# Attention and a gated feed-forward layer on one core: block means of the first batch's values from the windows of the first eight halves, with a new order list for the opening

## The chip, the cores and the metric

One core of one Trainium2 chip runs the kernel. Its engines are PE (matrix products; its weight loads are shown apart as PEld), DVE (vector), ACT (scalar functions), POOL (GpSimd) and SP, which here only issues transfers. The metric is the device time of one launch in microseconds (us), as a median over several runs. A hardware profile of one execution is at hand as well, and its span and rows are what the text argues from.

## The reference

Attention over 4 batches, 8 heads, 768 positions and 64 values a head. Every position sees a band of keys near it, and for each block of 32 positions one maximum of its keys and one mean of its values. The result passes through two dense layers with a rational function between them.

```python
k_sum = k.reshape(B, H, nb, block, D).max(axis=3)       # block = 32, nb = 24
v_sum = v.reshape(B, H, nb, block, D).mean(axis=3)
scores_l = where(|i - j| < 16, scale * q @ k.T, -1e9)
scores_s = scale * q @ k_sum.T + log(block)
a = softmax(concatenate([scores_l, scores_s], axis=-1))
x = a @ concatenate([v, v_sum], axis=2)
...
h = x @ w_in                                            # 3072 x 512 by 512 x 2048
P = a[0] + a[1] * h + a[2] * h**2 + a[3] * h**3
Q = 1.0 + |b[0]| * |h| + |b[1]| * h**2
out = (P / (Q + 1e-06)) @ w_out
```

## The kernel before

**Halves.** Attention works on 64 query positions of all eight heads at a time, a *half*; there are 48, twelve to a batch, and eight make the 512 rows of a *group* for the dense layers (six groups). A half uses a window of 96 keys and values (its 64 positions and 16 on either side) and the 24 block values of its batch, 120 rows in all. Its steps, in `half`, `softmax`, `turned` and `values`, are: scores on PE (`one_scores`, or `both_scores` for two halves at once where `PAIRS` has a 1), mask and minimum on DVE, exponentials on ACT, reciprocal on DVE, scaling on POOL, four transposes on PE (`turned`, with `FILL` matmuls without use ahead of them), a copy of the transposed rows (`ENG_P` says on which engine), the product with the values on PE, and the output split into a high part `xh` (`ENG_X`) and a rest `xl`.

**Names in the profile.** `sc` scores, `ss` attention rows, `sm` their minima and sums, `pt` and `pts` the transposed rows, `vw`, `vr` and `vlast` the value windows with their block means in rows 96 to 119, `av` the product, `vf` whole tiles of values and the sums over them, `kres` keys, `qres` queries, `ks` block maxima, `kw` the keys of one half, `wr` raw weights, `wearly` and `w` split weights, `h` the first layer's result, `ta`, `tq`, `tu`, `gh`, `gl` the rational function, `po` the second layer's result. `pt<-mask,ident` are the filling matmuls.

**Block means of the first batch.** The rows 96 to 119 of the eight windows of halves 0 to 7 (`vres`) hold the same 24 means. `value_tiles(0)` loads the batch's 768 value rows as six tiles of 128, in one transfer of four and one of two. Six accumulating matmuls (`value_average`, tokens v0 to v5) multiply them by the constant `avg`, which holds 1/32 in the right places. `first_means` (token m) copies the result into `vres`: three copies on ACT, five on POOL. The second batch's means are made in the same way (`u`, `n`). The windows themselves are loaded by `load_v` (tokens V).

**Steps.** A step is a first-layer block of 512 rows by 128 columns (`moe1`, tokens x, three parts of four matmuls), the rational function in nine parts (`gelu`, tokens ga to gk), and a second-layer part (`moe2`, tokens y). 96 steps make up the run, sixteen to a group. Weights come as 64-bit words and are turned into a high and a low part (`w_split`, tokens w).

**Order.** Up to first-layer step 13 the order is a list written out in `TEXT`. Each token advances one chain by one piece, and a wrapper around the engines makes each engine take its instructions in the order of the list. Capital letters issue loads from SP: K keys, Q queries, V value windows, F and G value tiles of the first and second batch, W weights, A queries and keys of later halves, I keys of the second batch; `S` loads the small constants. k and i make block maxima on DVE. After the list a loop goes on with steps 14 to 95.

Of the kernel before, what the change touches and what calls it, by code (L numbers as in the profile page):

```python
# [8 lines left out]
F32 = mybir.dt.float32  # L9
# [4 lines left out]
ALU = mybir.AluOpType  # L14
# [8 lines left out]
P = 128  # L23
# [24 lines left out]
TEXT = ("K0 K2 k0 K1 Q0 k1 k2 K3 k3 S0 Q1 F0 W0 V0 V1 V2 A9 V3 V5 V6 V7 W1 V4 W2 W3 h0 A8 G0 h0 h0 h1 h1 h0 h3 h1 h2 h0 h4 h6 h1 h2 h4 v0 h5 h0 h1 h1 h3 h4 h2 h0 h3 h6 h2 h2 h0 h2 "  # L48
# [11 lines left out]
AVGW = NK + NB - 4  # L60
NLATE = 4
# [6 lines left out]
PAIRS = "11001000"  # L68
SMODE = "xxxxxxxxxxxxxxxx"
ENG_P = "dddddaadaaaaaaaa"  # L70
ENG_X = "daadaaaaaaadaaaa"
MODE = "ccccceceeccccccc"
SQ_PS = "001001001001110"
PRODUCT = "00000000000000"
FILL = "0000000040200000"
TREE = "0000"
KDMA = "00000000"
# [4 lines left out]
def tile_kernel(ctx, tc, qw_in, kraw, kwin, vpad, vred, wio, a, b, cmask, cident, cavg, out):  # L82
# [52 lines left out]
    kfull = wm.tile([P, NPAIR * SPAD + AVGW], F32, tag="wm", name="kres")  # L135
    kres = kfull[:, 0:NPAIR * SPAD].rearrange("p (r s) -> p r s", r=NPAIR)
    avg = kfull[:, NPAIR * SPAD:]

# [52 lines left out]
    def value_tiles(bi):  # L191
        vt = []
        for i, (n, pool, tag) in enumerate(((4, xp, "xh"), (2, stage if bi else xp, "st" if bi else "xl"))):
            t = pool.tile([P, n, DM], F32, tag=tag, bufs=2, name=f"vf{bi}_{i}")
            syn.dma_start(out=t, in_=vpad[bi, WIN + 4 * i * P:WIN + (4 * i + n) * P, :].rearrange("(t p) e -> p t e", p=P))
            vt += [t[:, k, :] for k in range(n)]
        return vt

    order = {"v": 0, "m": 0}

    def value_average(av, vt, i):
        assert order["v"] % len(vt) == i
        order["v"] += 1
        pe.matmul(av[:NK, :], avg[:, AVGW - NK - 4 * i:AVGW - 4 * i], vt[i], start=(i == 0), stop=(i == len(vt) - 1))

    def first_means(av):
        assert order["v"] == 6
        order["m"] += 1
        for t in vres[0:3]:
            act.copy(t[NKW:NK, :], av[NKW:NK, :])  # L210
        for t in vres[3:]:
            gps.tensor_copy(t[NKW:NK, :], vw[0][NKW:NK, :])

    def second_means(av):
        order["m"] += 1
        t = pp.tile([NK, DM], F32, tag="p", name="vn")
        act.copy(t[NKW:NK, :], av[NKW:NK, :])
        syn.dma_start(out=vnext, in_=t[NKW:NK, :])
# [55 lines left out]
    def softmax(jj, sc):  # L274
# [31 lines left out]
        for pr in range(NPAIR):  # L306
            gps.tensor_scalar(ss[:, pr, 0:NK], ss[:, pr, 0:NK], sm[:, 1, pr:pr + 1], 1.0, op0=ALU.mult, op1=ALU.mult)
# [4 lines left out]
    def half(jj):  # L312

        other = jj ^ 1
        pair = PAIRS[jj // 2] == "1"
        if jj >= HPG:
            for k in (min(jj, other), max(jj, other)) if pair else (jj,):
                if k not in paired:
                    paired.add(k)
                    key_blocks(k)  # L320
            yield
        if jj not in score_tiles:
            if pair:
                score_tiles[min(jj, other)], score_tiles[max(jj, other)] = both_scores(min(jj, other))
            else:
                score_tiles[jj] = one_scores(jj)
            scored.update((jj, other) if pair else (jj,))
        yield
        yield from softmax(jj, score_tiles[jj])
        yield  # L330
        lead(turned(jj, jj < HPG), True)
        yield
        yield from values(jj, jj < HPG)

    def load_v(jj):
        bi, j = divmod(jj, NJ)
        vt = vres[jj] if jj < HPG else vw[jj % 2]
        assert jj < HPG + 2 or jj - 2 in finished
        syn.dma_start(out=vt[0:NKW, :], in_=vpad[bi, j * HQ:j * HQ + NKW, :])
        if j < 2 and bi == 1:  # L340
            assert order["m"] == 2
            syn.dma_start(out=vt[NKW:NK, :], in_=vnext)
        elif j < 2 and bi > 1:
            nc.gpsimd.dma_start(
                out=vt[NKW:NK, :].rearrange("n (q d) -> n q d", q=4),
                in_=vsum[bi].rearrange("p c e -> p (c e)"))

    finished, facing = set(), {}
# [307 lines left out]
    def token(kind, n):  # L656
# [29 lines left out]
        elif kind == "F":  # L686
            syn.dma_start(out=avg, in_=cavg)
# [3 lines left out]
        elif kind == "v":  # L691
            if n == 0:
                tiles["v"] = ps_a.tile([P, DM], F32, tag="a", name="vf")
            value_average(tiles["v"], tiles["f", 0], n)
        elif kind == "m":
            first_means(tiles["v"])
        elif kind == "u":
            if n == 0:
                tiles["u"] = ps_o.tile([P, DM], F32, tag="o", name="vf1")
            value_average(tiles["u"], tiles["f", 1], n)  # L700
# [49 lines left out]
def _layout(q, k, v, moe_w_in, moe_w_out, moe_a, moe_b):  # L750
# [27 lines left out]
    avg = np.zeros((P, AVGW), f)  # L778
    avg[np.arange(P), NKW + NB - 4 + np.arange(P) // BLK] = 1.0 / BLK
    return {  # L780
# [23 lines left out]
```

## Time and profile before

| what | value |
|---|---|
| median of three runs | 642.35 us (641.74 to 643.24) |
| the profiled execution | 641.28 us |
| its span | 639.5 us |
| PE busy | 621.2 us, 97% |
| DVE busy | 567.8 us, 89% |
| ACT busy | 460.2 us, 72% |
| POOL busy | 256.0 us, 40% |
| PE's granted clock | 1.00 |
| moved by DMA | 78.58 MB |

Busy times are unions of an engine's instructions. A row of the view of instructions in order of time gives start, duration, engine, line, operation, output and inputs, shape and count, and in brackets the idle time ahead and what ended it. Almost every row has the line of the wrapper, 110, so rows are told apart by their tiles. PE takes matmuls in a pipeline, so the distance between two starts, and not a duration, is what one costs there; an fp32 matmul shows as two.

### The profile page before, as it was taken

How to read it: one execution, taken by the hardware profiler on the slowest of the kernel's cores; microseconds unless marked ns; L12 is line 12 of the kernel's file. 1: busy time of each engine (PE TensorE's matmuls, PEld its weight loads, DVE VectorE, ACT ScalarE, POOL GpSimd, SP SyncE). 2: the span in 40 equal slices, each digit the busy share in tenths (PEclk: the TensorE clock that was granted, in tenths of full speed). 3: DMA queues.
4: the chain of work that ended last, by engine and by line, in shares of the span. 5: the costliest groups of instructions: out<-in, count | busy, mean ns of one | idle time of the engine just before them, and what ended most of it. 6: DMA issues, size and time to landing. Idle time of an engine off the chain costs nothing.

```text
span 639.5 us, 11900 instructions
## 1 busy us (share of the span) xinstructions
PE 621.2 (97%) x4080; PEld 497.0 (78%) x4080; DVE 567.8 (89%) x1152; ACT 460.2 (72%) x1032; POOL 256.0 (40%) x353
## 2 busy tenths in 40 slices
PE   8799999999999999999999999999999999999997
PEld 5566777778788878888888878888888888888886
DVE  5689989999989999989988989988988988898885
ACT  3989999978777767777767677667786775656652
POOL 1838768663243244243243234244234232222221
PEclk9999999999999999999999999999999999999999
DMA  9997856504534424333424442223342210100001
GB/s 319 302 353 259 260 161 207 193 27 138 164 122 140 132 81 139 114 114 127 143 79 121 123 145 89 86 92 98 86 143 85 72 64 1 55 12 2 0 2 66
DMA packets 52136, 78.58 MB, mean 123 GB/s; under 512 B 6132, under 2 KB 33396, under 8 KB 50156
## 3 DMA queue, kind: packets, MB, share of 16 engines
q1 hardware_dynamic: 50796, 75.67, 36.4%
q0 software_dynamic: 560, 1.77, 1.5%
q8 instruction: 32, 0.52, 0.3%
q10 hardware_dynamic: 720, 0.38, 0.2%
q14 instruction: 28, 0.23, 0.1%
HBM read 61.31 MB, written 14.73 MB: 119 GB/s over the span
## 4 chain that ended last, share of the span: by engine, by line
PE 72%; DVE 13%; ACT 6%; issue 3%; DMA 3%; POOL 2%; DVEq 0%; POOLq 0%; ACTq 0%
PE po L110 33%; PE h L110 31%; DVE tu L110 4%; PE sc L110 3%; DVE tq L110 3%; PE av L110 3%; ACT ta L110 2%; POOL ss L110 2%; DVE gh L110 2%; DMA kres<-in_kraw_dram 1%; ACT ss L110 1%; PE pt L110 1%; DVE vs L110 1%; DMA w<-wr 1%; PE vf L110 1%
## 5 line engine op out<-in xcount | busy, mean ns | idle before, releaser
L110 POOL TENSOR_TENSOR gl<-tu,ta 128x512 fp32r<-128x512 f32 x96 | 129.6, 1350 | 299.8 <-DVE tu L110 177.6
L110 ACT ACTIVATE ta<-tq,cs 128x512 f32<-128x512 f32 x96 | 69.6, 725 | 87.6 <-DVE tq L110 86.7
L110 PE MATMUL po<-wearly,gh 128*128 128x512 f32 x384 | 121.1, 397 | 0.9 <-ACT o L110 0.9
L110 POOL TENSOR_SCALAR ss<-ss,sm 128x120 f32<-128x120 f32 x192 | 94.6, 510 | 65.7 <-DVE sm L110 62.3
L110 PE MATMUL po<-w,gh 128*128 128x512 f32 x384 | 119.9, 394 | 0.0
L110 PE MATMUL h<-xh,wearly 128*128 128x512 f32 x384 | 97.4, 393 | 0.5 <-ACT xh L110 0.5
L110 PE MATMUL h<-xh,w 128*128 128x512 f32 x384 | 96.5, 391 | 1.3 <-DVE tu L110 1.0
L110 PEld LDWEIGHTS h<-xh,w 128*128 128x128 f32 x384 | 71.8, 188 | 16.9 <-ACT ta L110 1.4
L110 PEld LDWEIGHTS po<-wearly,gh 128*128 128x128 f32 x384 | 70.5, 188 | 18.2 <-ACT o L110 2.5
L110 PEld LDWEIGHTS h<-xh,wearly 128*128 128x128 f32 x384 | 71.9, 188 | 16.4 <-issue 0.7
L110 PEld LDWEIGHTS po<-w,gh 128*128 128x128 f32 x384 | 71.2, 188 | 15.6 <-issue 1.3
L110 DVE SCALAR_TENSOR_TENSOR gh<-tu,cs,ta 128x512 fp32r<-128x512 f32 x96 | 72.8, 759 | 11.7 <-ACT ta L110 2.2
L110 ACT ACTIVATE ss<-ss,sm 128x120 f32<-128x120 f32 x192 | 73.2, 384 | 12.7 <-DVE sm L110 12.5
L110 PE MATMUL po<-w,gl 128*128 128x512 f32 x192 | 75.0, 390 | 0.0
L110 PE MATMUL po<-wearly,gl 128*128 128x512 f32 x192 | 75.0, 390 | 0.0
L110 ACT ACTIVATE tu<-h,cs 128x512 f32<-128x512 f32 x96 | 74.6, 777 | 0.2 <-PE h L110 0.2
L110 DVE SCALAR_TENSOR_TENSOR tu<-tu,cs,tq 128x512 f32<-128x512 f32 x96 | 72.2, 752 | 2.7
L110 DVE SCALAR_TENSOR_TENSOR tu<-tu,cs,h 128x512 f32<-128x512 f32 x96 | 71.1, 740 | 2.2
L110 DVE SCALAR_TENSOR_TENSOR tq<-tq,gh 128x512 f32<-128x512 f32 x96 | 67.0, 698 | 2.7
L110 ACT ACTIVATE ta<-h,cs 128x512 f32<-128x512 f32 x96 | 65.2, 679 | 5.1 <-POOL gl L110 5.1
L110 DVE TENSOR_TENSOR tu<-tu,h 128x512 f32<-128x512 f32 x96 | 64.9, 676 | 1.2 <-ACT tu L110 0.7
L110 ACT ACTIVATE ta<-ta 128x512 f32<-128x512 f32 x96 | 60.8, 633 | 2.7
(78 smaller groups left out, 911.0 us busy)
## 6 DMA issues: line engine op xcount, KB each, us to landing
wr<-in_wio_dram SPq DMA_DIRECT2D x15, 1024.0 KB
cross<-tb SPq DMA_DIRECT2D x32, 256.0 KB
vw<-in_vpad_dram SPq DMA_DIRECT2D x42, 192.0 KB
kw<-in_kwin_dram SPq DMA_DIRECT2D x40, 192.0 KB
pts<-cross SPq DMA_DIRECT2D x96, 64.0 KB
out_dram<-o SPq DMA_DIRECT2D x23, 256.0 KB
qw<-in_qw_dram SPq DMA_DIRECT2D x40, 128.0 KB
kr<-in_kraw_dram SPq DMA_DIRECT2D x12, 384.0 KB
```

Of the source, the lines that this page charges most:

```text
L110: out = getattr(self.engine, name)(*args, **kw)
```

## The change

The first batch's means come from ten matmuls in place of six. Eight take rows 16 to 79 of the windows of halves 0 to 7, once loaded (`window_average`, tokens v0 to v7, with a constant `avgw` of 96 rows); two take the last two whole tiles (`value_average`, v8 and v9), the only ones that are still loaded. `first_means` makes two copies on ACT and six on POOL.

Other settings change with it. `PAIRS`: halves 4 to 7 score in pairs too. `SMODE`: half 1 subtracts its minimum on POOL, takes one exponential for all four blocks and sums on DVE (y); halves 2 to 5 are scaled on DVE by one product over all four blocks (z). `ENG_P`, `ENG_X`: which engine copies. `SQ_PS`: the square of step 1 goes to PSUM. `PRODUCT`: step 0 forms its denominator with two ACT operations and a POOL product. `FILL`: fewer filling matmuls. `KDMA`: the block maxima of half 12 are copied by a transfer. The order list is another one; of it the openings are shown, to about the first x tokens.

```diff
-TEXT = ("K0 K2 k0 K1 Q0 k1 k2 K3 k3 S0 Q1 F0 W0 V0 V1 V2 A9 V3 V5 V6 V7 W1 V4 W2 W3 h0 A8 G0 h0 h0 h1 h1 h0 h3 h1 h2 h0 h4 h6 h1 h2 h4 v0 h5 h0 h1 h1 h3 h4 h2 h0 h3 h6 h2 h2 h0 h2 "
-         "h3 v1 h3 h3 h5 h4 h5 h4 w0 v2 v3 w0 w0 h7 h4 v4 v5 h3 h5 h7 m0 h2 h1 h0 h2 h5 h1 h1 h0 h0 w0 h5 w0 W4 h6 h3 h6 h7 h7 h4 h6 h4 h2 h6 h7 h2 h7 h1 h2 h1 h5 h5 h3 h6 h3 h5 w1 "
...
+TEXT = ("K0 K2 K1 Q0 K3 Q1 k2 V2 k0 V0 F0 V5 S0 k1 V1 k3 h0 h0 W0 V6 h1 V4 h0 V3 h0 h1 V7 W1 A8 h1 A9 h2 h0 h4 h3 h2 h3 v0 v2 h3 h4 h0 h1 h2 h2 h0 h3 h1 h2 v1 h6 h5 h3 h2 w0 W3 h3 "
+         "W2 v5 h4 h6 v9 G0 h0 h5 w0 h4 h4 v8 h1 w0 v6 v4 h5 h5 h4 v3 h7 v7 h1 m0 h0 h5 h2 h5 h7 h7 h3 h1 h2 w0 w0 h6 h0 h0 h6 h6 h4 h3 h2 h2 h7 h1 h1 h2 h6 h5 h5 h3 h5 h3 h7 h1 h4 "
...
+AVGH = NK + NB - 2
+NREST = (S - HPG * HQ) // P
-PAIRS = "11001000"
-SMODE = "xxxxxxxxxxxxxxxx"
-ENG_P = "dddddaadaaaaaaaa"
-ENG_X = "daadaaaaaaadaaaa"
+PAIRS = "11111000"
+SMODE = "xyzzzzxxxxxxxxxx"
+ENG_P = "dddddaadaaaaaada"
+ENG_X = "addaadaaaaddaaaa"
-SQ_PS = "001001001001110"
-PRODUCT = "00000000000000"
-FILL = "0000000040200000"
+SQ_PS = "011001001001110"
+PRODUCT = "10000000000000"
+FILL = "0000000010000010"
-KDMA = "00000000"
+KDMA = "00011000"
+ENG_M = "aagggggg"
...
-        for i, (n, pool, tag) in enumerate(((4, xp, "xh"), (2, stage if bi else xp, "st" if bi else "xl"))):
+        for i, (k, n, pool, tag) in enumerate(((0, 4, xp, "xh"), (4, 2, stage, "st")) if bi else ((S // P - NREST, NREST, xp, "xl"),)):
...
+    def window_average(av, n, jj):
+        assert jj in loaded
         order["v"] += 1
-        pe.matmul(av[:NK, :], avg[:, AVGW - NK - 4 * i:AVGW - 4 * i], vt[i], start=(i == 0), stop=(i == len(vt) - 1))
+        pe.matmul(av[:NK, :], avgw[:, AVGH - NK - 2 * jj:AVGH - 2 * jj], vres[jj][0:NKW, :], start=(order["v"] == 1), stop=(order["v"] == n))
...
-        for t in vres[0:3]:
-            act.copy(t[NKW:NK, :], av[NKW:NK, :])
-        for t in vres[3:]:
-            gps.tensor_copy(t[NKW:NK, :], vw[0][NKW:NK, :])
+        for t, e in zip(vres, ENG_M):
+            if e == "a":
+                act.copy(t[NKW:NK, :], av[NKW:NK, :])
+            else:
+                (dve if e == "d" else gps).tensor_copy(t[NKW:NK, :], vw[0][NKW:NK, :])
...
-        for pr in range(NPAIR):
+        if jj < 2 * HPG and SMODE[jj] == "z":
+            dve.tensor_tensor(ss, ss, sm[:, 1, :].unsqueeze(2).to_broadcast([P, NPAIR, NK]), op=ALU.mult)
+        for pr in range(NPAIR) if jj >= 2 * HPG or SMODE[jj] != "z" else ():
             gps.tensor_scalar(ss[:, pr, 0:NK], ss[:, pr, 0:NK], sm[:, 1, pr:pr + 1], 1.0, op0=ALU.mult, op1=ALU.mult)
...
-            syn.dma_start(out=avg, in_=cavg)
+            syn.dma_start(out=kfull[:, NPAIR * SPAD:], in_=cavg)
```

More of the change, by code (lines that the diff above doesn't have):

```diff
@@ L134, in tile_kernel @@
     qres = wm.tile([P, HPG, NPAIR, HQ], F32, tag="wm", name="qres")
-    kfull = wm.tile([P, NPAIR * SPAD + AVGW], F32, tag="wm", name="kres")
+    kfull = wm.tile([P, NPAIR * SPAD + AVGW + AVGH], F32, tag="wm", name="kres")
     kres = kfull[:, 0:NPAIR * SPAD].rearrange("p (r s) -> p r s", r=NPAIR)
     avg = kfull[:, NPAIR * SPAD:]
+    avgw = kfull[0:NKW, NPAIR * SPAD + AVGW:]
     def setup():
@@ L192, in value_tiles, with value_average @@
         vt = []
-        for i, (n, pool, tag) in enumerate(((4, xp, "xh"), (2, stage if bi else xp, "st" if bi else "xl"))):
+        for i, (k, n, pool, tag) in enumerate(((0, 4, xp, "xh"), (4, 2, stage, "st")) if bi else ((S // P - NREST, NREST, xp, "xl"),)):
             t = pool.tile([P, n, DM], F32, tag=tag, bufs=2, name=f"vf{bi}_{i}")
-            syn.dma_start(out=t, in_=vpad[bi, WIN + 4 * i * P:WIN + (4 * i + n) * P, :].rearrange("(t p) e -> p t e", p=P))
-            vt += [t[:, k, :] for k in range(n)]
-        return vt
-    order = {"v": 0, "m": 0}
-    def value_average(av, vt, i):
-        assert order["v"] % len(vt) == i
+            syn.dma_start(out=t, in_=vpad[bi, WIN + k * P:WIN + (k + n) * P, :].rearrange("(t p) e -> p t e", p=P))
+            vt += [(k + c, t[:, c, :]) for c in range(n)]
+        return vt
+    order = {"v": 0, "m": 0, "u": 0}
+    def value_average(kind, av, n, k, vt):
+        order[kind] += 1
+        pe.matmul(av[:NK, :], avg[:, AVGW - NK - 4 * k:AVGW - 4 * k], vt, start=(order[kind] == 1), stop=(order[kind] == n))
+    def window_average(av, n, jj):
+        assert jj in loaded
         order["v"] += 1
-        pe.matmul(av[:NK, :], avg[:, AVGW - NK - 4 * i:AVGW - 4 * i], vt[i], start=(i == 0), stop=(i == len(vt) - 1))
+        pe.matmul(av[:NK, :], avgw[:, AVGH - NK - 2 * jj:AVGH - 2 * jj], vres[jj][0:NKW, :], start=(order["v"] == 1), stop=(order["v"] == n))
     def first_means(av):
-        assert order["v"] == 6
+        assert order["v"] == HPG + NREST
         order["m"] += 1
-        for t in vres[0:3]:
-            act.copy(t[NKW:NK, :], av[NKW:NK, :])
-        for t in vres[3:]:
-            gps.tensor_copy(t[NKW:NK, :], vw[0][NKW:NK, :])
+        for t, e in zip(vres, ENG_M):
[3 more added lines that the diff above has]
+                (dve if e == "d" else gps).tensor_copy(t[NKW:NK, :], vw[0][NKW:NK, :])
     def second_means(av):
+        assert order["u"] == S // P
         order["m"] += 1
@@ L322, in half @@
         if jj not in score_tiles:
+            assert jj >= HPG or order["k", 0] == NPAIR
             if pair:
@@ L338, in load_v @@
         assert jj < HPG + 2 or jj - 2 in finished
+        loaded.add(jj)
         syn.dma_start(out=vt[0:NKW, :], in_=vpad[bi, j * HQ:j * HQ + NKW, :])
@@ L346, in load_v @@
                 in_=vsum[bi].rearrange("p c e -> p (c e)"))
-    finished, facing = set(), {}
+    finished, loaded, facing = set(), set(), {}
     def turned(jj, early=False):
@@ L691, in token @@
         elif kind == "v":
-            if n == 0:
+            if order["v"] == 0:
                 tiles["v"] = ps_a.tile([P, DM], F32, tag="a", name="vf")
-            value_average(tiles["v"], tiles["f", 0], n)
+            if n < HPG:
+                window_average(tiles["v"], HPG + NREST, n)
+            else:
+                value_average("v", tiles["v"], HPG + NREST, *tiles["f", 0][n - HPG])
         elif kind == "m":
@@ L697, in token @@
         elif kind == "u":
-            if n == 0:
+            if order["u"] == 0:
                 tiles["u"] = ps_o.tile([P, DM], F32, tag="o", name="vf1")
-            value_average(tiles["u"], tiles["f", 1], n)
+            value_average("u", tiles["u"], S // P, *tiles["f", 1][n])
         elif kind == "n":
@@ L777, in _layout @@
         ms.append(np.concatenate([m, m], axis=0))
-    avg = np.zeros((P, AVGW), f)
+    avg = np.zeros((P, AVGW + AVGH), f)
     avg[np.arange(P), NKW + NB - 4 + np.arange(P) // BLK] = 1.0 / BLK
+    rows = np.arange(HQ)
+    avg[WIN + rows, AVGW + NKW + NB - 2 + rows // BLK] = 1.0 / BLK
     return {
```

20 rows, old and new, of the table TEXT are left out of this document.

## The prediction, on record before the changed kernel was timed

> **What bounds the kernel now.** I read the page's span first, then the busy times by stage, then who PE waited for in each stage, then the instructions of each engine in order of time.
>
> ```profile
> span 639.5 us, 11900 instructions
> ...
> 9.00:36.86 27.86, 22.89 (x428) 17.05 (x429) 19.48 (x93) 21.92 (x86) 20.03 (x41) 1.00 1.04 339
> 36.86:139.50 102.64, 98.21 (x613) 73.13 (x614) 98.26 (x193) 94.10 (x188) 68.01 (x61) 1.00 0.65 209
> 139.50:639.50 500.00, 492.86 (x3029) 403.82 (x3027) 446.77 (x864) 342.91 (x758) 167.76 (x248) 1.00 0.29 91
> ```
>
> The columns after the length are the busy times of PE, PEld, DVE, ACT and POOL, then PE's granted clock, the DMA share and GB/s. The order list ends near 139.5 us. Behind it PE is busy for 492.86 of 500.00 us, by code that the change leaves alone. So the change can act in two stages only. **Stage A**, 9.00 to 36.86, is the attention of the first eight halves, up to the first first-layer matmul. No engine is full there: PE idles 27.86 - 22.89 = 5.0 us. **Stage B**, 36.86 to 139.5, interleaves first-layer steps 0 to 13 and second-layer steps 0 to 10 with eight more halves. There PE is busy 98.21 of 102.64 us and DVE 98.26. Both are 96% full and ACT 92%, so taking work from one of them alone need not shorten it.
>
> ```profile
> PE pt L110 <- DVE pts L110: 1.2, 1, 1.2
> ...
> PE av L110 <- DVE xl L110: 0.8, 2, 0.5
> ...
> PE pt L110 <- POOL ss L110: 3.1, 6, 0.9
> PE h L110 <- DVE tu L110: 1.0, 1, 1.0
> ```
>
> The first two rows are waits of PE in stage A (total, times, longest), both for attention's small DVE work. The last two are those of stage B, mostly for POOL scaling the attention rows.
>
> **The change, part by part.** First PE's terms.
>
> ```profile
> 9.04 0.40 PE L110 MATMUL sc<-kres,qres 64*64 64x96 f32 x8 [0.29 <-DMA qres<-in_qw_dram]
> 9.31 0.40 PE L110 MATMUL sc<-kres,qres 64*64 64x96 f32 x8
> ...
> 18.62 2.74 PE L110 MATMUL vf<-vf,kres 128*120 128x512 f32 x6
> 21.29 0.38 PE L110 MATMUL sc<-kres,qres 64*64 64x96 f32 x4
> 21.59 0.36 PE L110 MATMUL sc<-kres,qres 64*64 64x96 f32 x4
> ...
> 51.65 2.58 PE L110 MATMUL pt<-mask,ident 128*128 128x360 f32 x8
> 54.07 0.38 PE L110 MATMUL pt<-ident,ss 128*120 128x128 f32 x2
> 55.33 0.66 PE L110 MATMUL pt<-ident,ss 128*120 128x128 f32 x2 [0.88 <-POOL ss L110]
> ```
>
> The means of batch 0 take ten matmuls (eight windows of 96 rows, two whole tiles) where six stood. Each is two passes of 512 columns; six passes took 21.29 - 18.62 = 2.67, so 0.445 a pass and four more matmuls cost 8 x 0.445 = +3.6 us. No row shows one of 96 rows. By rows they would be 0.75 of it, which makes all ten 2 x 0.445 x (2 + 8 x 0.75) = 7.1 against 5.3 now, +1.8; the upper end is +3.6 with nothing gained for fewer rows. I take +3.6, by the row of equal columns. Halves 4 to 7 now score in pairs: a block of eight passes over the keys and eight over the block maxima takes 9.31 - 9.04 = 0.27 for two halves at once, against 21.59 - 21.29 = 0.30 for four and four of one half alone. A half alone is four such blocks, 1.2 us; a pair is 4 x 0.27 = 1.1. Two pairs in place of four singles save 4 x 1.2 - 2 x 1.1 = 2.6. So PE has +3.6 - 2.6 = +1.0 in stage A. The filling matmuls of the turns fall from six (four at half 8, two at half 10) to two (one at 8, one at 14). Eight passes took 54.07 - 51.65 = 2.42, 0.30 each, so four fewer save 8 x 0.30 = 2.4 in stage B. The four at half 8 now stand in front of a wait that went on for another 0.88 after them, so their removal pays only if the list has other PE work to put there.
>
> Next the engines beside it.
>
> ```profile
> 19.69 1.39 POOL L110 TENSOR_SCALAR ss<-ss,sm 128x120 f32<-128x120 f32 x4 [0.19 <-DVE sm L110]
> ...
> 25.27 1.73 POOL L110 COPY vr<-vw 24x512 f32<-24x512 f32 x3 [0.47 <-ACT vw L110]
> ...
> 30.76 2.75 POOL L110 TENSOR_SCALAR ss<-ss,sm 128x120 f32<-128x120 f32 x8 [0.21 <-DVE sm L110]
> ...
> 51.68 3.93 POOL L110 TENSOR_SCALAR ss<-ss,sm 128x120 f32<-128x120 f32 x4
> ...
> 49.24 0.68 DVE L110 TENSOR_TENSOR tu<-tu,h 128x512 f32<-128x512 f32 x1
> 49.84 0.75 DVE L110 SCALAR_TENSOR_TENSOR tq<-tq,cs,ta 128x512 f32<-128x512 f32 x1
> 50.50 0.74 DVE L110 SCALAR_TENSOR_TENSOR tu<-tu,cs,h 128x512 f32<-128x512 f32 x1
> ...
> 58.09 0.95 DVE L110 TENSOR_REDUCE ks<-kr 128x24 f32<-128x768 f32 x1
> 58.96 0.17 DVE L110 RECIPROCAL sm<-sm 128x4 f32<-128x4 f32 x1
> ...
> 27.86 0.42 DVE L110 CAST xh<-av 128x256 fp32r<-128x256 f32 x1
> 29.90 0.68 DVE L110 COPY pts<-pt 120x512 f32<-120x512 f32 x1
> 39.38 0.32 DVE L110 COPY kw<-ks 128x96 f32<-128x96 f32 x2
> ...
> 24.55 1.06 ACT L110 COPY vw<-vf 24x512 f32<-24x512 f32 x2 [0.93 <-PE vf L110]
> ...
> 30.34 0.19 ACT L110 ACTIVATION_READ_ACCUMULATOR ss<-ss,sm 128x1 f32 x1
> ```
>
> Scaling a half costs POOL 1.39 (four instructions, DVE quiet). Halves 2 to 5 give this to DVE as one product of 128x480. The nearest row, 128x512, starts 0.60 before the next, so I take 0.6 each: DVE +2.4, POOL -4 x 1.39 = -5.6. Half 1 subtracts its minimum on POOL in one instruction (between 0.3, one of the four scalings, and 1.4, all four; I take 1.3, as it covers all four blocks), ACT takes one exponential in place of four with their accumulator reads, and DVE gets a reduction of 480 columns (0.95 for 768, so 0.59) and an addition on four (0.17 as the reciprocal), 0.75; ends 0.34, two of the short ones, and 1.1 (0.95 + 0.17). One mean copy moves from ACT to POOL (1.73 / 3 = 0.58). Three output copies (halves 1, 2, 5) move to DVE and two (0, 3) away, net one of 0.42. So in stage A, DVE has +2.4 + 0.75 + 0.4 = +3.5, with 27.86 - 19.48 = 8.4 idle to hold it; POOL has -5.6 + 1.3 + 0.6 = -3.7.
>
> Where stage A ends is set by the last halves. Now their scalings end at 30.76 + 2.75 = 33.5, and the first layer starts 3.35 later, at 36.86. In the new list PE makes all ten averaging matmuls before the second transpose; I put their end where it is now, near 24.6, since PE has +1.0 more but idles less ahead of it. Then come two ACT copies (24.55 + 1.06 shows them), six POOL copies of 0.58, to about 24.6 + 0.5 + 3.5 = 28.6, and then the scalings of halves 6 and 7. The last exponential stands behind as much ACT work as now and ends near 30.5 (its last read is at 30.34), so half 7 is scaled from 30.5 and done by 31.9 to 32.9 (1.4 alone, up to 2.4 beside a busy DVE). That is 0.6 to 1.6 earlier; I take **-1.1**. What is late next is the ACT and DVE pair of output copies of halves 6 and 7, as now.
>
> Stage B has two ends. If PE sets it, it shrinks by the 2.4 of fills. If DVE sets it, it grows by DVE's own balance: step 0's combination moves to POOL, 49.84 to 50.50, -0.66; one copy of block maxima goes by DMA, 0.32 / 2, -0.16; half 14's transposed copy and half 10's output copy come to it, 0.68 + 0.42; together +0.3. I take **-0.8**, between them: PE's waits here are for POOL (3.1) three times as much as for DVE (1.0), and the list puts first-layer work of step 4 ahead of the first second-layer work, near where the fills stood, which speaks for PE's end; DVE's 98.3 speaks for the other.
>
> Edits that I cost at nothing. The loads:
>
> ```profile
> wr<-in_wio_dram SPq DMA_DIRECT2D x6, 1024.0 KB
> vf<-in_vpad_dram SPq DMA_DIRECT2D x2, 1024.0 KB
> kres<-in_kraw_dram SPq DMA_DIRECT2D x4, 400.0 KB
> qres<-in_qw_dram SPq DMA_DIRECT2D x2, 512.0 KB
> vf<-in_vpad_dram SPq DMA_DIRECT2D x2, 512.0 KB
> vr<-in_vpad_dram SPq DMA_DIRECT2D x4, 192.0 KB
> ...
> 374.76 1.98 DMA cross<-tb
> ...
> 36.14 1.89 POOL L110 TENSOR_SCALAR wr<-wr 128x1024 int32<-128x1024 uint8 x1 [0.17 <-DMA wr<-in_wio_dram]
> ```
>
> Batch 0 drops its 1024 KB tile, some 3.1 us of transfer at the 339 GB/s of stage A. What it relieves is the weights, and the wait for those is 0.17; so nothing is booked. SP's queue takes value windows 2, 0, 5 and 1 ahead of the first weights and the others right behind. The averages now wait for all eight, and behind that wait stand PE's transposes. Ahead of the last window lie keys, queries, eight windows, two tiles and one weight block: 4 x 400 + 2 x 512 + 8 x 192 + 512 + 1024 KB = 5.8 MB, 17.2 us at 339 GB/s. Begun near 2 us and with 1.98 for a landing (the row of a small transfer) at most, they are there by 21.2, while PE reaches the last average near 23.7. The cover is 2.5 us; gone, the means and all behind them come later by what is lacking. The block maxima of half 12 by DMA add an issue on SP, where weights and windows queue behind its wait for the maxima, and a landing of some 1.98; both are covered if the scores stand that far behind, and the loads behind it are several steps early. Step 1's square in PSUM changes the buffer, not the operation.
>
> Sum: -1.1 - 0.8 = -1.9. The profiled execution took 641.28, its span 639.5 and 1.8 around it, so it would come to 639.4. It lies 1.1 below the median of the runs, 642.35, and I forecast a median of **640.4**.
>
> **A rule weighed.** POOL's four scalings took 1.39 at 19.69 and 3.93 at 51.68, where DVE was full: one slows the other. The Trainium skill, SBUF — State Buffer, "SBUF: two separate sides", says that GpSimd and a VectorE operation with two SBUF inputs take the shared port in turn, whole instructions long. The POOL rows agree. By it, the four products on DVE may each wait out a POOL copy, and moving work between those two need not help; the rival of no change below prices this from rows.
>
> **The rivals.** (1) *PE takes it all*: the list fills the waits, stage B gives the 2.4 of fills and most of the 3.1 of POOL waits. With stage A that is -1.1 - 2.4 - 2 = -5.5, 636.9. For it: POOL loses 3.7 early. Against it: DVE's 98.3 of 102.6. Chance 0.12. (2) *No change, the products collide*: the four scalings on DVE wait for POOL copies of 0.58 each, 4 x 0.58 = 2.3 on the path that now hands pairs of halves to PE; -1.9 + 2.3 = +0.4, 642.8. For it: 1.39 against 3.93. Against it: POOL is mostly done with early scalings then. Chance 0.24. (3) *Slower, DVE becomes the bound of both stages*: its queue is in order, and the scalings of halves 2 and 3 stand behind the reciprocals of 1, 2 and 3, so it idles for ACT's exponentials and then runs late; the added 3.5 of stage A lies wholly on the path, with nothing back in B. That is 642.35 + 3.5 = 645.9. It decides if DVE's 8.4 of idle time in stage A can't be used, that is if less than 3.5 of it remains after those reciprocals. Against it: the fewer accumulator reads and the pairs start the later softmaxes sooner. Chance 0.16.
>
> **How the numbers follow.** The forecast has 0.48, with its own range 639.0 to 641.8. What a measurement can tell from no change is 0.2%, 1.3 us: faster is below 641.1, slower above 643.6. Of the forecast 0.41 lies below and 0.07 within. Rival 1 gives 0.12 to faster, rival 2 0.05, 0.16 and 0.03, rival 3 0.16 to slower. Together 0.58, 0.23 and 0.19. For 8 in 10 I go from 637.2, which leaves out half of rival 1, to 644.2, which leaves out most of rival 3.
>
> **What would show it.** In the new profile: the first first-layer matmul near 35.8 us; ten averaging matmuls at 0.445 a pass; four DVE products of about 0.6 on 128x480; POOL below 17 us busy in stage A; the list's end (first first-layer matmul of step 14) near 137.6; PE's waits for POOL's scaling in stage B below 3; everything behind as long as now, 500 us. Wrong would be: averages that wait for a window, a first first-layer matmul after 37 us, or a stage B in which DVE stays full and PE's gaps grow by what the fills gave.

## The result, and the profile after

The changed kernel takes 646.33 us (median of six runs, 645.69 to 650.12) against 641.8 for the kernel before on the same chip: a ratio of 1.0078, 95% interval 1.0052 to 1.0105. (Ratios here are worked out from all the runs and are not the quotient of the two medians.) It is slower, above the forecast of 640.4 and outside the range of 637.2 to 644.2. The profiled execution took 645.69, its span 643.9 where before had 639.5.

The changed kernel by stage (same columns as before): stage A, stage B up to the list's end, and all behind it.

```profile
9.00:36.79 27.79, 24.49 (x438) 16.41 (x437) 22.36 (x98) 20.90 (x77) 15.06 (x27) 1.00 1.04 360
36.79:143.25 106.46, 98.19 (x605) 73.11 (x606) 97.96 (x193) 92.14 (x185) 65.60 (x62) 0.97 0.59 186
143.25:643.90 500.65, 493.29 (x3029) 403.53 (x3027) 448.28 (x864) 343.12 (x758) 168.34 (x248) 1.00 0.29 91
```

Stage A is 27.79 us long instead of 27.86, stage B 106.46 instead of 102.64 and the rest 500.65 instead of 500.00. So +3.8 of the +4.4 lies in stage B, and there PE's granted clock is 0.97 instead of 1.00. Who PE waited for in stage B (total, times, longest):

```profile
PE h L113 <- DMA wearly<-wr: 3.9, 2, 3.5
PE h L113 <- DMA w<-wr: 1.3, 1, 1.3
...
PE pt L113 <- POOL ss L113: 0.7, 2, 0.5
```

The wait for POOL's scaling fell from 3.1 to 0.7, as the change does it. New are 5.2 us of waits for transfers, and one of 3.5 alone. PE's instructions around that wait (start, length, group, idle time before it and what ended it), first of the kernel before, then of the changed one:

```profile
74.28 0.39 PE L110 MATMUL po<-wearly,gl 128*128 128x512 f32 x1
74.51 1.07 PE L110 MATMUL h<-xh,wearly 128*128 128x512 f32 x4
75.41 0.62 PE L110 MATMUL po<-wearly,gh 128*128 128x512 f32 x2
```

```profile
75.91 2.08 PE L113 MATMUL h<-xh,wearly 128*128 128x512 f32 x4 [3.47 <-DMA wearly<-wr]
77.78 1.05 PE L113 MATMUL po<-wearly,gh 128*128 128x512 f32 x2
...
81.20 0.52 PE L113 MATMUL po<-wearly,gl 128*128 128x512 f32 x1
81.55 0.62 PE L113 MATMUL h<-xh,wearly 128*128 128x512 f32 x2
```

These four matmuls are the last third of first-layer step 5, with the low part of weight block 5. Before, PE reached them at 74.51 and did not wait. Now it reaches them at 75.91 - 3.47 = 72.44 and idles. What follows is slow as well: the four take 77.78 - 75.91 = 1.87 us instead of 75.41 - 74.51 = 0.90. The nine second-layer matmuls behind take 81.55 - 77.78 = 3.77; where the clock stays at 1.00, nine such take 2.04 (shown below, with block 5 on DVE). The clock of that stretch:

```profile
60.00:80.00 20.00, 16.15 (x105) 12.23 (x100) 15.81 (x37) 15.38 (x31) 11.23 (x13) 0.87 0.80 236
80.00:100.00 20.00, 19.22 (x132) 14.61 (x131) 17.74 (x41) 17.51 (x38) 12.27 (x12) 0.96 0.60 168
```

The low part that PE waits for comes from an accumulating transfer. For most blocks DVE subtracts the high part from the weights. For blocks 5, 7 and 8 (an "e" in `MODE`, in both kernels) ACT writes the negated high part, and POOL issues a 512 KB transfer that adds the weights to it. The changed kernel's critical chain runs through it (start, length, what):

```profile
65.67 0.96 ACT wearly L113
66.63 0.62 ACT ta L113
67.25 0.00 issue
67.25 8.61 DMA wearly<-wr
75.87 0.04 issue
75.91 2.08 PE h L113 x4
```

It was issued at 67.25, and at 67.85 before. So the issue isn't late; the landing is. Time from issue to landing of blocks 5 and 7, shortest, median and longest, of the kernel before and then of the changed one:

```profile
DMA to landing us min/median/max: 4.6/5.0/5.4
```

```profile
DMA to landing us min/median/max: 6.0/7.3/8.6
```

Landed after 5.4 us, the part would have been there at 72.65, 0.2 after PE wanted it. What the transfer met is seen on SP's queue: the 1024 KB load of weight block 8, issued at 60.96 before and at 66.92 now, 0.33 us ahead of the transfer.

```profile
60.96 0.35 SPq L110 DMA_DIRECT2D wr<-in_wio_dram  x1
```

```profile
66.92 0.37 SPq L113 DMA_DIRECT2D wr<-in_wio_dram  x1
```

By the packets of the trace, the transfer's first one left 3.83 us after its issue, when 112 of the load's 128 had left; in the kernel before it left after 1.67 us, with the load long done.

### The profile page after: what moved, and what is told of

The parts are those of the page before. It is cut to its first block, busy times and chain, and to the rows that moved or that the text cites. A ratio compares the mean times of both kernels' runs of the same rounds, so it can differ in the third digit from the quotient of the medians.

```text
span 643.9 us, 11880 instructions
## 1 busy us (share of the span) xinstructions
PE 623.5 (97%) x4080; PEld 496.2 (77%) x4080; DVE 572.0 (89%) x1159; ACT 457.4 (71%) x1020; POOL 249.2 (39%) x340
## 4 chain that ended last, share of the span: by engine, by line
PE 67%; DVE 13%; ACT 8%; DMA 7%; issue 3%; POOL 3%; DVEq 0%; ACTq 0%; POOLq 0%
PE po L113 32%; PE h L113 30%; DVE tu L113 3%; DVE tq L113 3%; PE av L113 3%; PE sc L113 2%; ACT ss L113 2%; ACT ta L113 2%; POOL ss L113 2%; DMA wr<-in_wio_dram 2%; DVE gh L113 2%; DMA kres<-in_kraw_dram 1%; DMA wearly<-wr 1%; DMA w<-wr 1%; DMA vnext<-vn 1%
## 5 line engine op out<-in xcount | busy, mean ns | idle before, releaser
L113 POOL TENSOR_SCALAR ss<-ss,sm 128x120 f32<-128x120 f32 x176 | 83.0, 492 | 52.2 <-DVE sm L113 51.4
L113 DVE SCALAR_TENSOR_TENSOR gh<-tu,cs,ta 128x512 fp32r<-128x512 f32 x96 | 74.1, 772 | 16.3 <-ACT sq L113 3.4
L113 ACT ACTIVATE ss<-ss,sm 128x120 f32<-128x120 f32 x188 | 71.7, 386 | 11.1 <-DVE sm L113 10.9
```

The lines of the kernel that those rows point to most:

```text
L113: out = getattr(self.engine, name)(*args, **kw)
```

## The experiments

A chip's runs of the kernel before gave medians of 641.3 to 641.8; each ratio is against those beside it. "Stage A" and "stage B" are of the one profiled execution, which need not be near the median.

**The means alone, and the means undone.** Old list and settings, ten averaging matmuls, the 1024 KB tile no longer loaded, and window 4 loaded ahead of weight block 1:

```diff
 # the changed kernel's code with the settings and the list of before
-W1 V4 .. v0 .. v1 .. v2 v3 .. v4 v5
+V4 W1 .. v8 .. v9 .. v0 v1 .. v2 v3 v5 v6 v7 v4
```

> The kernel before, its settings and its list, with the means alone changed: ten averaging matmuls in place of six, window 4 loaded ahead of weight block 1, one load of 1024 KB gone, three copies of the means on ACT and five on POOL as before. Theory (the loss is the late transfer's and the means cost little): stage A grows by up to the 3.6 of matmuls, less what the earlier loads give, and the time is 0 to 3 above before, 642 to 645. Rival (the averages wait for the windows and this is the whole loss): 4.4 or more above, 646 or more, with PE's averages waiting for a window's load.

645.46, ratio 1.0061 [1.0046, 1.0076]. Its windows by stage:

```profile
9.00:40.60 31.60, 26.30 (x437) 18.55 (x437) 20.19 (x94) 21.85 (x86) 20.22 (x41) 1.00 0.97 328
40.60:143.20 102.60, 98.11 (x612) 73.07 (x613) 98.23 (x193) 94.14 (x188) 68.02 (x61) 1.00 0.59 190
```

Stage A ends 3.7 later and stage B is as before. PE's busy time in stage A grew by 26.30 - 22.89 = 3.4 and its idle time by 0.3, so in the old order the four more matmuls (3.6) lie wholly on the path. The other way round, six whole tiles again in the new list with the early load of block 8 (next experiment):

```diff
-((S // P - NREST, NREST, xp, "xl"),)
+((0, 4, xp, "xh"), (4, 2, xp, "xl"))
-v0 .. v9 (windows, two tiles)
+v0 .. v5 (six tiles), in the last six places
```

> The changed kernel with the early load of weight block 8, and the means of batch 0 again from six tiles of values (six averaging matmuls, at the last six of the ten places in the list, and the 1024 KB load back). Theory (the four more matmuls lie on the path of stage A, as the 3.7 that the means cost alone in the old list say): stage A ends 1.5 to 3.6 earlier, near 35, and the time falls below the early load alone by as much, to 638.5 to 640.6. Rival (the loads are the path: a further 1024 KB ahead of the windows and the first weights): stage A ends as late or later, 642 or more.

645.61, ratio 1.0078 [1.005, 1.0105], 3.5 above the early load alone. ACT waits 6.3 us for the first weights, as 1024 KB more goes ahead of them, and stage A ends at 41.3. That is the profile of the longest of five runs (650.61), and it has a granted clock of 0.84 in stage A and 0.97 in stage B; the other four stand at 0.988 to 0.993. So the loads and the clock are mixed here, and means and list can't be priced one by one.

**The load of block 8 earlier.**

```diff
-V10 .. V11 W8
+W8 V10 .. V11
```

> The changed kernel with one token moved: the load of weight block 8 stands ahead of value window 10 in the list, some 6 us earlier, so that it is no longer in flight when block 5's accumulating transfer is issued. Theory (the accumulating transfer queues behind that load, PE waits 3.47 us for it and then runs at half clock for some 5.6 us): the transfer lands in 5.0 to 5.6 us in place of 8.6, PE's wait for it falls below 0.5, the granted clock between 60 and 80 us is 1.00 again, and the time falls by about 6, to some 640 us. Rival (the slowness is DVE's, full in both stages, and the wait only shows it): the wait moves to another place and the time stays within 1.5 us of 646.3. Rival (the transfer is slow by itself): it still lands in 8 us or more, no change.

642.15, ratio 1.001 [0.9992, 1.0028]: this one move gives the loss back, as the interval takes in 1. Its waits in stage B, and PE at step 5:

```profile
PE h L111 <- DMA wearly<-wr: 2.5, 2, 1.5
PE h L111 <- DMA w<-wr: 1.7, 1, 1.7
```

```profile
75.77 1.19 PE L111 MATMUL h<-xh,wearly 128*128 128x512 f32 x4 [1.50 <-DMA wearly<-wr]
76.80 0.62 PE L111 MATMUL po<-wearly,gh 128*128 128x512 f32 x2
...
78.63 0.39 PE L111 MATMUL po<-wearly,gl 128*128 128x512 f32 x1
78.86 1.07 PE L111 MATMUL h<-xh,wearly 128*128 128x512 f32 x4
```

The transfer's first packet leaves 1.76 us after issue. The wait is 1.50 instead of 3.47, and the nine second-layer matmuls behind it take 78.86 - 76.80 = 2.06 instead of 3.77. Stage B is 102.7. Two marks were missed: the transfer landed after 6.7 us, not 5.0 to 5.6, and the wait did not fall below 0.5. Four of the nine runs still stand at a clock of 0.995 to 0.997.

**Other work ahead of the late part.** Second-layer parts of steps 1 and 2 before the last third of step 5:

```diff
-x5 gi4 i3 y1 ga5 y2 h11 gj4 gb5 y2 h12
+gi4 i3 y1 y2 h11 gj4 y2 x5 ga5 gb5 h12
```

> The changed kernel with three second-layer parts (9 matmuls, 2.04 us) that stood behind the last third of first-layer step 5 put ahead of it, and that step's first two function parts behind it. The transfer is left as late as it was. Theory with the clock (an idle stretch of 3.5 us costs a further 2.7 by half clock): idle falls to 1.4, the clock stays at 1.00, the time falls by 2.0 + 2.7 = 4.7, to 641.6. Theory without the clock: only the 2.0 of filled wait come back, 644.3. Rival (DVE is the bound): less than 1.

644.68, ratio 1.0058 [1.0034, 1.0081]; stage B 104.6. The transfer landed after 9.5 us, so PE still waited 1.90 where 1.4 was expected, and six of the ten runs stand at a clock of 0.995 to 0.997: the median can't tell the two theories apart. With the early load as well:

> The changed kernel with both moves: weight block 8 loaded early, and three second-layer parts ahead of the last third of first-layer step 5. Theory (late accumulating transfers are the loss of stage B): the wait at step 5 (3.47 us in the changed kernel, 1.50 with the early load alone) goes to 0, so 1 to 1.5 less than the early load alone, 640.5 to 641.2. Rival (DVE is the bound from there on): as the early load alone, 642.1, with the wait found again at a DVE operation.

641.7, ratio 1.0006 [0.9993, 1.0019]. In its profile, of one of the long runs (643.89), the wait at step 5 is down to 0.15, but one of 1.84 for block 8 opens later; the two edits don't add.

**The load put late in the old kernel.** Two tries to make the delay where the list is the old one, with the load on ACT's queue:

```diff
-W8 (SP's queue, issued 60.96)
+W8 behind w5's negation (act.dma_start)
```

> The kernel before with the load of weight block 8 moved from 60.96 us to just ahead of block 5's accumulating transfer (issued from ACT's queue, to come at that time). Theory (the accumulating transfer shares its way with a load issued just ahead of it): its landing goes from 4.6 to 5.4 to some 8.5 us, past the 74.5 at which PE wants it; PE waits 1 to 2 us, below the length at which its clock fell; the time rises by 1 to 2. Rival (the landing does not depend on the load): 5 us still, no change.

641.54, ratio 0.9997 [0.9987, 1.0008], landing 4.7 to 5.6: a miss. ACT's issue ran ahead of its arithmetic, at 65.60, 2.0 us before the transfer.

```diff
+W8 behind half 9's copy of the transposed rows (act.dma_start)
```

> The kernel before, with the load of weight block 8 (1024 KB) taken off SP's queue and issued by ACT right behind the copy of half 9's transposed rows, near 67.4 us: half a microsecond ahead of POOL's accumulating transfer of weight block 5 (67.85), as in the changed kernel, where they stand 0.3 us apart. In the earlier try the load stood 2.0 us ahead and nothing changed. Theory 1 (an accumulating transfer that is issued just behind such a load starts behind it): it lands in 7.5 to 8.6 us instead of 5.4, PE waits 1 to 2 us for the early weights at step 5 (none now), and the median is 643 to 645. Theory 2 (the changed order alone makes the wait; the load is chance): landing near 5.5, no new wait, 641.5 to 642.5. If PE then waits 2 us or more and the granted clock of the next 5 us drops below 0.9, the clock drop belongs to the wait and not to the changed kernel.

641.29, ratio 0.9997 [0.9988, 1.0006]: again ahead, at 65.98, and the transfer landed after 5.8 instead of 5.4. Its first packet left 2.13 us after issue, as the load ended. This fits a transfer that starts when the load is nearly out. A delay of 3 us was not made on the old kernel, but other profiles repeat it. In the early-load kernel, block 8's transfer was issued at 91.97, 1.16 us behind another 1024 KB load whose packets left from 91.76 to 95.32, and its first packet left 3.76 us after its issue. In two other versions (parts of steps 1 and 2 first, above, and the one with PE kept busy, below) block 8's load was issued 0.1 us *behind* block 5's transfer, and the transfer's first packet left after 4.97 and 5.00, with 115 and 116 of the load's 128 gone. So the delay goes with a load in flight, not with which of the two was issued first. Whether DVE, busy behind these issues, has a part in it was not tested.

**The transfer taken away, the load left.** One letter:

```diff
-MODE = "ccccceceeccccccc"
+MODE = "ccccccceeccccccc"
```

> The changed kernel with the low part of weight block 5 made by DVE's subtraction, as for most blocks, instead of ACT's negation and POOL's accumulating transfer; nothing else is moved, the load of block 8 stays where the change put it. DVE takes about 1.2 us more, ACT 1.0 less. Theory 1 (the late transfer makes PE's 2.08 us wait at step 5, and the wait makes the clock drop behind it): no wait for early weights at step 5, granted clock above 0.99 from 60 to 100 us, stage B from 106.5 to 103 or 104, median 642 to 643.5. Theory 2 (stage B is long because DVE or ACT are late there, the transfer only shows it): PE waits for DVE's subtraction or the rational function instead, stage B stays above 105, median 645 to 647. Theory 3 (the clock drop comes with the new order and not from the wait): no wait, but the clock still below 0.95 between 60 and 100 us, median 644 to 646.

(The 2.08 us that it names are the four matmuls' length; the wait is 3.47.) 640.74 us, ratio 0.9999 [0.9985, 1.0013], 0.8% or some 5 us below the changed kernel by the ratios. Its windows by stage, and PE where the wait was:

```profile
9.00:37.60 28.60, 25.39 (x439) 16.54 (x437) 22.87 (x98) 20.88 (x77) 15.06 (x27) 1.00 1.04 351
37.60:138.20 100.60, 96.16 (x605) 71.23 (x606) 99.19 (x194) 91.38 (x184) 66.78 (x61) 1.00 0.59 193
138.20:637.80 499.60, 492.64 (x3029) 403.68 (x3027) 445.29 (x864) 343.62 (x758) 167.75 (x248) 1.00 0.29 91
```

```profile
73.14 1.07 PE L113 MATMUL h<-xh,wearly 128*128 128x512 f32 x4
74.05 0.62 PE L113 MATMUL po<-wearly,gh 128*128 128x512 f32 x2
...
75.86 0.39 PE L113 MATMUL po<-wearly,gl 128*128 128x512 f32 x1
76.09 1.07 PE L113 MATMUL h<-xh,wearly 128*128 128x512 f32 x4
```

No wait at step 5, clock 1.00, and the nine matmuls take 76.09 - 74.05 = 2.04. Stage B is 100.6. Theory 1, and more than it expected.

**The wait made in the old kernel.** The negation of block 5 later, so that the transfer is issued at 72.69 instead of 67.85; load and order else as before:

```diff
-h11 w5 i2 w5 x4 h9 w5 gd3 .. gb4 ge4
+h11 w5 i2 x4 h9 gd3 .. gb4 w5 w5 ge4
```

> The kernel before, with ACT's negation of weight block 5 moved behind its second operation on step 4's result, and POOL's accumulating transfer behind that: issued near 71.9 us instead of 67.85, landing near 77.3, while PE wants the part at 74.5. Nothing else is changed. So PE should wait 2.5 to 3 us at step 5 in the old kernel as well. Theory 1 (the wait itself brings the clock drop, in whatever order): granted clock below 0.95 in the 20 us behind it, median 644.5 to 646.5, that is the wait and 2 us more. Theory 2 (the drop needs something else of the changed kernel): clock 1.00, and the median rises by no more than the wait, 642.5 to 644.5; other work of stage B's idle time may take some of it back.

645.45 in five runs of 645.35 to 645.99, ratio 1.0068 [1.0056, 1.008]. Waits, PE at the place, and two windows of 3.41 us, the second from where the clock drops to where it comes back:

```profile
PE h L108 <- DMA wearly<-wr: 2.6, 1, 2.6
```

```profile
77.50 1.21 PE L108 MATMUL h<-xh,wearly 128*128 128x512 f32 x4 [2.60 <-DMA wearly<-wr]
78.55 0.93 PE L108 MATMUL po<-wearly,gh 128*128 128x512 f32 x2
...
81.83 0.53 PE L108 MATMUL po<-wearly,gl 128*128 128x512 f32 x1
82.19 1.37 PE L108 MATMUL pt<-mask,ident 128*128 128x360 f32 x4
```

```profile
75.29:78.70 3.41, 1.20 (x5) 1.01 (x6) 3.41 (x7) 2.85 (x4) 3.31 (x4) 1.00 0.67 115
78.70:82.12 3.42, 3.42 (x10) 2.67 (x9) 3.38 (x6) 1.17 (x2) 2.01 (x2) 0.50 0.83 331
```

A wait of 2.60 costs about 4 us in the old kernel too: the four matmuls take 78.55 - 77.50 = 1.05 and the nine behind them 82.19 - 78.55 = 3.64, together 1.7 more than the 0.90 and 2.05 of the kernel before. The loss needs neither the new means nor the new list, only a late transfer that PE waits for.

**PE kept busy in the wait.** The eight matmuls of step 5's first two thirds, two more times ahead of the last third; only the last pass counts:

```diff
+if g == 0 and fc == 5 and k == 2 * NCC:
+    for _ in range(2): (the eight matmuls again, from start=True)
```

> The changed kernel with the first two thirds of first-layer step 5 computed three times over, the last one counting: 16 matmuls more, 3.6 us of PE work without use, all of it inside the wait of 3.5 us. The wait's end does not move. Theory with the clock: PE is not idle, so the nine second-layer matmuls behind the wait take 2.05 in place of 3.77 and the first-layer part 0.91 in place of 1.87, and the time falls by 2.5 to 2.7, to 643.7. Theory without the clock: no change or 0.2 more, 646.3 to 646.5.

The wait is 0.2, the clock 0.999 or 1.000 in all four runs and stage B 103.4 instead of 106.5, so without idle PE there was no drop. Yet the median is 646.73, ratio 1.0078 [1.0062, 1.0093]: the order of the instructions behind the list is not written out but planned when a kernel is built, it changed too, and from step 14 to step 32 PE took 113.8 us instead of 111.7. As a price of the drop it is spoilt.

**What is left.** All of these start from the early load or from block 5 on DVE.

```diff
-SMODE = "xyzzzzxxxxxxxxxx"
+SMODE = "xyxxxxxxxxxxxxxx"     # with the early load
```

> The changed kernel with the early load of weight block 8, and the scaling of halves 2 to 5 back on POOL. Theory (DVE's 2.4 lies in its idle time, and POOL's early scalings kept the means' copies waiting): stage A ends 0 to 2 later, time 642 to 644. Rival (DVE is the bound of stage A, or the products collide with POOL's copies): stage A ends earlier by 1 or more and the time falls below 641.

643.48, ratio 1.0035 [1.002, 1.0051]; the early load alone has 1.001 [0.9992, 1.0028]. The intervals overlap, but a fall of more than about 0.5 us would lie outside them, so the products on DVE are not what costs. Its profile is of the shortest run (640.75).

```diff
 # with the early load: high part, negation and transfer of blocks 5, 7 and 8, 4 to 12 places up (block 5 shown)
-gj2 ga3 gb3 gk2 h9 h10 w5 .. gf3 h9 h11 w6 W8 V10 w5 I3 x4 A12 w5
+gj2 w5 ga3 gb3 gk2 h9 h10 .. gf3 w5 h9 h11 w5 w6 W8 V10 I3 x4 A12
```

> The changed kernel with the early load of weight block 8, and in its order list the high parts, the negations and the accumulating transfers of weight blocks 5, 7 and 8 moved up by 4 to 12 places, some 1 to 2 us each. In the early-load kernel PE waited 2.5 us for two of these transfers and 1.7 us for the third. Theory 1 (lateness of these transfers sets stage B): the waits shrink below 1.5 in total, stage B goes from 102.7 to about 100, and the median from 642.15 to about 639.5. Theory 2 (ACT and DVE are full in stage B, and what is moved ahead there makes the rational function late instead): stage B stays at 102 to 103, PE waits for ta, tu or gl instead, and the median is 641.5 to 643.

644.09, ratio 1.0046 [1.0033, 1.0059]. The profiled run has stage B at 101.8; three of five runs stand at a clock of 0.997 and 644.1 to 645.4. A miss.

```diff
 # with the early load: the first three operations on weight block 0 behind half 5's exponentials
-w0 W3 .. h5 w0 h4 h4 v8 h1 w0 v6 v4 h5 h5 h4 v3 .. h2 h5 h7
+W3 .. h5 h4 h4 v8 h1 v6 v4 h5 h5 w0 h4 w0 v3 .. h2 h5 w0 h7
```

> The changed kernel with the early load of weight block 8, and the three first operations on weight block 0 (ACT's, POOL's and DVE's) moved behind the exponentials of half 5, so that ACT doesn't wait for that load (3.0 us in the changed kernel's profile, 4.1 in the early-load kernel's) with the exponentials of halves 4 and 5 queued behind it. Theory 1 (that wait holds stage A back): halves 4 to 7 are scaled about 2 us earlier, the first first-layer matmul comes near 35.5 instead of 36.8 to 38.6, and the median is 640 to 641. Theory 2 (stage A's end is set by weight block 0 itself, whose split then ends later, or by the mean copies on POOL): it stays at 36.8 to 38.6, PE waits for early weights instead of for transposed rows, and the median stays within 0.5 of 642.15.

642.19, ratio 1.0013 [0.9995, 1.0032]; stage A 37.2. All of it together:

> The changed kernel with all edits that gave a shorter stage in a profile: the early load of weight block 8, the weight operations of block 0 behind half 5's exponentials (first first-layer matmul 37.2 instead of 38.6), the accumulating transfers of blocks 5, 7 and 8 moved up (stage B 101.8 instead of 102.7), and second-layer parts of steps 1 and 2 ahead of the last third of step 5. Theory 1 (the parts add, and with no wait above 1 us no clock drop is left): stage A to 37.2, stage B 100 to 101, clock at or above 0.999 in every run, median 639 to 640.5, below both kernels. Theory 2 (the new list depends on when single loads land, so another wait opens in its place): runs spread over 4 us, some at a clock of 0.997 and these 2 us longer, median 641.5 to 643.5.

642.9, ratio 1.0034 [1.0015, 1.0054]. Theory 2: the parts, each taken from one profile, don't add. Eight of eleven runs stand at a clock of 0.989 to 0.997.

```diff
-MODE = "ccccceceeccccccc"
+MODE = "cccccccccccccccc"      # all three blocks on DVE
+MODE = "cccccccecccccccc"      # blocks 5 and 8
```

> The changed kernel with the low parts of weight blocks 5, 7 and 8 all made by DVE; no accumulating transfer is left in the opening. With block 5 alone the median was 640.74, and of its twelve runs the four with a granted clock of 0.997 were the long ones by 1 to 4 us. Theory 1 (the clock drops left there come from waits for the transfers of blocks 7 and 8): no run below 0.999, spread under 2 us, median 639.5 to 640.5. Theory 2 (DVE is the bound once it takes 2.4 us more): stage B from 100.6 to 102 or 103, PE waits for DVE's tu, median 641.5 to 643.

> The changed kernel with blocks 5 and 8 on DVE and block 7 left on the accumulating transfer. Theory 1: the wait at block 8 (0.4 us in the profile with block 5 alone on DVE, more in its long runs) goes, and most of the 0.997 runs with it: median 639.8 to 640.5. Theory 2 (DVE's 1.2 us more lie on the path): median 641 to 642.

643.12, ratio 1.0038 [1.0022, 1.0054], and 641.51, ratio 1.0001 [0.9993, 1.001]. With 5 and 8 on DVE, all eleven runs have a clock of 0.999 or 1.000 and lie within 2.0 us. But with one, two and three blocks on DVE stage B takes 100.6, 101.6 and 102.7 in these profiles, about 1 us a block: beyond the first, what a block on DVE spares is spent again. With all three on DVE four of nine runs still stand at 0.997, though no accumulating transfer is left in the opening; so those drops have another cause, which no profile caught.

> The changed kernel with block 5 on DVE, and the three first operations on weight block 0 moved behind half 5's exponentials. Theory 1 (ACT's wait for the first weights costs stage A up to 1.4 us, as the earlier pair of profiles had it, 38.6 against 37.2): first first-layer matmul at 36 to 37.2 instead of 37.6, median 639.5 to 640.2. Theory 2 (stage A ends where it does for other reasons, and that pair showed only its jitter of 36.8 to 38.6): 37 to 38, median 640.5 to 641.5.

640.47, ratio 0.9993 [0.9979, 1.0007], stage A 37.3: theory 2. No version is below the kernel before by more than its interval.

## Why the prediction was wrong

**The step that failed** is the edits "that I cost at nothing". It says of the weights' loads that "what it relieves is the weights, and the wait for those is 0.17; so nothing is booked", and of the loads behind the block maxima of half 12 that they "are several steps early". That looked at what the loads feed. It didn't ask what they run beside: the queues that a moved load is moved past. The new list moves block 8's load 6 us later, to 0.33 us ahead of a transfer on POOL's queue, and lets PE reach that transfer's result 74.51 - 72.44 = 2.1 us sooner. The lines needed stood in the profile of before: the transfer's 5.4 us and its cover. It landed at 67.85 + 5.4 = 73.2, PE wanted it at 74.51, so 1.3 us of cover was left, and the prediction never set it against the 2.4 of fills that it took from PE just there. No rival named it either. Rival 3 gave nearly the measured time, 645.9, by another mechanism: DVE's 3.5 of stage A on the path. Stage A ended no later (36.79 against 36.86), and in stage B DVE took 97.96 us against 98.26, so that is not what happened; the nearness is chance.

**The second thing left out** is the clock. The rows of before show 1.00 in all stages and I took it as fixed. The slow stretch costs (1.87 - 0.90) + (3.77 - 2.04) = 2.7 us, on top of the wait's 3.47.

**Stage B, -0.8.** Mended in one letter (one block's subtraction on DVE instead of the transfer), it came to 100.6, -2.0. PE's busy time there is 96.16 instead of 98.21, and its idle time the same 4.4. So the fills' 2.4 came out at PE's end and DVE's balance did not set it: the term was too small, and its sign right. PE's waits for POOL fell below 3, as predicted.

**Stage A, -1.1.** It gave nothing. The terms of PE stand: 24.49 against 22.89 is +1.6 where +1.0 was summed, and ten averaging matmuls of 96 or 128 rows alike go at 0.43 to 0.475 a pass. DVE took +2.9 (predicted 3.5), POOL -5.0 (predicted -3.7). What failed is the end of the chain. PE, then POOL, in the changed kernel:

```profile
24.46 1.02 PE L113 MATMUL vf<-vlast,kres 96*120 96x512 f32 x2
25.32 0.60 PE L113 MATMUL pt<-ident,ss 128*120 128x128 f32 x4
...
36.78 0.50 PE L113 MATMUL h<-xh,wearly 128*128 128x512 f32 x1 [0.47 <-ACT xh L113]
```

```profile
20.92 1.15 POOL L113 TENSOR_SCALAR wr<-wr 128x1024 int32<-128x1024 uint8 x1 [5.82 <-DMA wr<-in_wio_dram]
...
26.28 2.34 POOL L113 COPY vr<-vw 24x512 f32<-24x512 f32 x4 [2.73 <-ACT vw L113]
28.57 2.17 POOL L113 COPY vlast<-vw 24x512 f32<-24x512 f32 x2
30.83 2.75 POOL L113 TENSOR_SCALAR ss<-ss,sm 128x120 f32<-128x120 f32 x8
```

The averages end at 25.3, not 24.6. The six mean copies were to take 3.5 us and took 30.74 - 26.28 = 4.5, the two on `vlast` 1.08 each. So the last scalings end at 33.58, where they ended before (33.51). Ahead of this, ACT waited for the first weights with two halves' exponentials behind it:

```profile
ACT wr L113 <- DMA wr<-in_wio_dram: 3.0, 1, 3.0
```

Taking that wait away did not shorten the stage by more than its scatter: nine profiles with the same stage A code end it between 36.8 and 38.6, 37.5 on average, and the three with the first weights' operations moved end it at 37.2, 37.3 and 37.9. The 36.8 of the changed kernel's own profile is the earliest of the nine. Four profiles with the old stage A end it between 36.6 and 37.1, so the new one is, if anything, some 0.7 us longer. In the longest of the nine PE waited 1.7 us for a value window, with the 2.5 us of cover that I gave it gone:

```profile
PE vf L111 <- DMA vw<-in_vpad_dram: 1.7, 1, 1.7
```

**The rest, 500 us "by code the change leaves alone".** 500.65: its order is planned anew with each kernel, and some of DVE's instructions behind the list stand elsewhere than before. It came to 499.6 with block 5 on DVE; that this half microsecond either way comes from the order is likely and not shown.

**Rival 2, products that collide,** is out: it asks for some 2.3 us back with the four scalings on POOL again, and the median did not fall.

## What to carry to other kernels

Where a list moves, write down for every transfer whose result PE waits for: issue, landing, first use, and the loads issued in the few microseconds ahead of it. Making PE quicker uses up cover; here 1.3 us of it lay under a gain of 2. A wait of PE that long is not the whole price: 3.47 us brought 2.7 of slow matmuls behind it, 2.60 brought 1.7.

## What the runs showed of the hardware

PE's granted clock in these traces is 1.00 or 0.50, and it changes only at steps of 3.41 us. In the changed kernel it is at half for two steps, from 74.63 to 81.46:

```profile
71.22:74.63 3.41, 1.22 (x6) 0.67 (x4) 3.41 (x13) 3.35 (x7) 2.79 (x2) 1.00 0.99 214
74.63:78.04 3.41, 2.13 (x5) 1.75 (x6) 0.87 (x2) 0.37 (x2) 1.39 (x4) 0.50 0.45 118
78.04:81.46 3.42, 3.42 (x9) 2.65 (x9) 2.49 (x4) 3.42 (x8) 0.00 (x0) 0.50 0.62 261
```

With the wait of 2.60 in the old kernel it is at half for one step (78.70 to 82.12, above). One step at half clock, full of matmuls, loses 3.41 / 2 = 1.7 us, which is the 1.7 behind that wait. Of the two steps here 1.28 us is still the wait, so (6.83 - 1.28) / 2 = 2.8 is lost, near the 2.7 measured. Over 640 us one such step shows as a mean clock of 0.997 and two as 0.995. All six runs of the changed kernel stand at 0.992 to 0.997; with block 5 on DVE eight of twelve stand at 1.000, and of its runs above 642 us both are at 0.997.

The length of a wait alone does not say whether the clock drops: it did with waits of 3.47, 2.60, 2.33, 1.84 and even 1.65 us (the version with all parts together), and did not with 1.97 (blocks 5 and 8 on DVE), 1.90 and 1.50. How the wait lies to the steps counts. Each step between 9 us and the list's end in which PE was busy for less than 1.3 of the 3.41 us was followed by half clock (1.22 and 1.20 in the rows here, 1.11 in the one with six whole tiles in the new list); between 1.5 and 2.0 either came, and the 1.97 us wait lay across two steps with 2.04 and 2.81 busy. That is from single profiles, and the exact rule is open. The Trainium skill, TensorE: Matmul & The Clock Gate, "What's actually happening", says that a free-running window of about 3.4 us sets the clock to half after one idle window and back after a busy one. The steps of 3.41 us agree, and so does the return after a full one. That PE must be idle for the whole of it they do not bear out: 1.22 us of work did not hold the clock, and the 2.60 us wait brought the drop in all five runs.

An accumulating transfer on POOL's queue with a 1024 KB load issued 0.3 us ahead of it sent its first packet 3.83 us after its issue, instead of 1.67, and landed after 8.6 us instead of 5.4. The Trainium skill, DMA: Bandwidth & Descriptors, "Queues, rings and completion order", says that each DMA engine takes its queues in turn, packet by packet. Here the two shared the engines only in the last of the load's 128 packets, which is 8 for each of the 16 engines if they are spread evenly. The same section of the Trainium skill counts about 9 to 17 descriptors to a typical packet, and the trace does not tell whether its own packets are those or single descriptors; so whether the rule holds here is open.
